# Two of the first four token tiles of x transposed by DMA instead of by TensorE

## The chip, the cores and the metric

The kernel runs on one core of a Trainium2 chip. The metric is the device time of one execution in microseconds (us); the time of the kernel before is the median of four runs, 180.27 us (180.03 to 180.73). A difference below about 0.3% (0.54 us) is not told from no change here.

## The reference

The inputs are in bf16: x with 2048 tokens of 512 features, wqkv (512 x 1536), wo (512 x 512), w1 and w3 (512 x 1376), w2 (1376 x 512) and gate_w (512). A linear-attention block and a gated feed-forward block work on the same x, and a gate per token mixes them:

```python
phi = lambda t: where(t > 0, t + 1, exp(t)) + 1e-6
q, k, v = heads(x @ wqkv)                       # 32 heads of 16
pq, pk = phi(q), phi(k)
kv = einsum("bhsd,bhse->bhde", pk, v)           # over all tokens
z = pk.sum(tokens)
a = (pq @ kv) / (pq . z + 1e-6) @ wo
b = (silu(x @ w1) * (x @ w3)) @ w2
g = sigmoid((x * gate_w).sum(-1))
out = g * a + (1 - g) * b
```

## The kernel before

The tokens are 16 tiles of 128 (t = 0 to 15), in four blocks of four tiles (`tb` = 0 to 3, `TB` = 512 tokens, `TPB` = 4). The 512 features are four chunks of 128 (`KC` = 4).

x is held twice in the on-chip memory. `x_sb` is token-major: a token's row lies in one partition. `xT` is feature-major: partition d of chunk kc holds feature kc*128+d of all tokens. A projection (k, q, the feed-forward) contracts over features and so reads `xT`. The product `XP` = x-transposed times phi(k), from which kv is made later, contracts over tokens and so reads `x_sb`.

All loads but one are issued by SP's queue, in the order of the program (L83 to L112). Before anything else come the token-major tiles 0-1 (L83), the second half of wk (L85; the first half goes by ACT's queue, L84) and the token-major tiles 2-3 (L86). Then, for each of the blocks 1 to 3, one DMA that reads 512 rows of x and writes them transposed into `xT` (L90), and one plain DMA that loads the same four tiles into `x_sb` (L94). After these come the weights wq, wr (the remainder of w1 and w3, and gate_w), wv, w1, w3, wo and w2 (L97 to L112). SP issues one after the other. Later SP issues small transposing DMAs between on-chip buffers (`hTr` L271: 128x128; `pqT` L295: 128x512, four of each per block), and the stores.

Block 0's `xT` isn't loaded. `emit_xT(t)` makes it for one tile: four 128x128 transposes on TensorE (PE, L174) into PSUM, then a copy of two chunks by VectorE (DVE, L179) and of two by ScalarE (ACT, L181).

Tiles 0-1, and tiles 2-3, are loaded in pairs: partition p of a pair holds the tokens 2p and 2p+1 of its 256 tokens, so that each partition's part is one run of 2 KB (`x_pairs`). The tokens of a pair of tiles therefore stand in another order in `x_sb`, `xT` and everything made from them, and the stores of tiles 0 to 3 put them back (`out_pairs`, L369).

TensorE's instructions are kept in the order of the program (L150). That order is: warm-up matmuls (L161); `emit_xT(0)` and `emit_xT(1)`; six matmuls of k for tiles 0 and 1 (L377); `emit_xT(2)` and `emit_xT(3)`; the ten matmuls left of k for tiles 1 to 3 (L382 to L385). Then, for t = 4 to 15 (L390 to L394), the four XP matmuls of tile t-4 alternate with the four k matmuls of tile t: XP(0), k(4), XP(1), k(5), XP(2), k(6) and so on. After k the q projections, the attention's small matrices, and the feed-forward blocks with the output matmuls follow to the end.

After each k tile comes `phi` (ACT L140, DVE L142 and L145) into `pk_sb`, and POOL adds the tile to a running sum (L192, L194). The four PSUM buffers of k ("mm") are taken again in turn, so k(4) needs what phi(k) of tile 0 leaves free.

Of the kernel before, what the change touches and what calls it, by code (L numbers as in the profile page):

```python
# [17 lines left out]
def kernel(  # L18
# [13 lines left out]
    P = nc.NUM_PARTITIONS  # L32
# [7 lines left out]
    TB = 512  # L40
    NTB = S // TB
    TPB = TB // P
# [6 lines left out]
    x2d = A_x.flatten_outer_dims()  # L49
    out2d = out.flatten_outer_dims()  # L50
# [13 lines left out]
    x_sb = consts.tile([P, NT, D], BF16, name="x_sb")  # L64
    xT = consts.tile([P, KC, S], BF16, name="xT")
# [12 lines left out]
    w3_r = B_w3.rearrange("(kc d) f -> d kc f", d=P)  # L78
    x_r = x2d.rearrange("(t p) d -> p t d", p=P)
    dq = nc.sync  # L80
    x_pairs = x2d[0:TB, :].rearrange("(g p j) d -> g p j d", p=P, j=2)
    out_pairs = out2d[0:TB, :].rearrange("(g p j) d -> g j p d", p=P, j=2)
    dq.dma_start(out=x_sb[:, 0:2, :], in_=x_pairs[0])  # L83
    nc.scalar.dma_start(out=wk_sb[:, 0:2, :], in_=wqkv_r[:, 0:2, D : 2 * D])  # L84
    dq.dma_start(out=wk_sb[:, 2:4, :], in_=wqkv_r[:, 2:4, D : 2 * D])  # L85
    dq.dma_start(out=x_sb[:, 2:TPB, :], in_=x_pairs[1])  # L86
    pre = consts.tile([1, 1], FP32, name="pre")
    nc.scalar.activation(out=pre[:], in_=nc.const_aps.tensor(0.0, [1, 1], FP32), func=ACT.Exp)
    for tb in range(1, NTB):
        dq.dma_start(  # L90
            out=xT[:, :, tb * TB : (tb + 1) * TB], in_=x2d[tb * TB : (tb + 1) * TB, :],
            transpose=True,
        )
        dq.dma_start(  # L94
            out=x_sb[:, tb * TPB : (tb + 1) * TPB, :], in_=x_r[:, tb * TPB : (tb + 1) * TPB, :]
        )
    dq.dma_start(out=wq_sb[:], in_=wqkv_r[:, :, 0:D])  # L97
    dq.dma_start(out=wr_sb[:, :, 0:FR], in_=w1_r[:, :, FM:F])
    dq.dma_start(out=wr_sb[:, :, FR : 2 * FR], in_=w3_r[:, :, FM:F])
    with nc.allow_non_contiguous_dma(reason="one gate weight per partition and chunk"):  # L100
        dq.dma_start(
            out=wr_sb[:, :, 2 * FR : NR], in_=gate_w.rearrange("(kc d o) -> d kc o", d=P, o=1)
# [7 lines left out]
    for fcs in (slice(0, FC // 2), slice(FC // 2, FC)):  # L110
# [9 lines left out]
        out=bm, in_=bm, pattern=[[-Dh, HPC], [0, Dh]], compare_op=ALU.is_ge, fill=0.0,  # L120
# [3 lines left out]
        out=bm, in_=bm, pattern=[[Dh, HPC], [0, Dh]], compare_op=ALU.is_ge, fill=0.0,  # L124
# [44 lines left out]
    def emit_xT(t):  # L169
        for h in range(2):  # L170
            xTp = psX.tile([P, 2, P], BF16, tag=f"XP{(2 * t + h) % 4}", name="xTp")
            for j in range(2):
                kc = 2 * h + j
                nc.tensor.transpose(  # L174
                    out=xTp[:, j, :], in_=x_sb[:, t, kc * P : (kc + 1) * P], identity=ident[:]
                )
            xT_t = xT[:, 2 * h : 2 * h + 2, t * P : (t + 1) * P]
            if h == 0:
                nc.vector.tensor_copy(out=xT_t, in_=xTp[:])  # L179
            else:  # L180
                nc.scalar.activation(out=xT_t, in_=xTp[:], func=ACT.Copy)  # L181
# [7 lines left out]
    def emit_k_phi(k_ps, t):  # L189
        e_ins = phi(pk_sb[:, t, :], k_ps[:])  # L190
        if t == 0:
            nc.gpsimd.tensor_copy(pks[:], pk_sb[:, t, :])  # L192
        else:
            nc.gpsimd.tensor_add(pks[:], pks[:], pk_sb[:, t, :])  # L194
# [137 lines left out]
    def emit_out(tb, tt):  # L332
        t = tb * TPB + tt
        tsl = slice(tt * P, (tt + 1) * P)

        if t < NT - 1:
            parts = [(0, D, True)]
        else:
            h, q3 = D // 2, 3 * D // 4
            parts = [(0, h, True), (h, q3, False), (q3, D, True)]  # L340
        o_out = work.tile([P, D], BF16, tag="o_out", name="o_out")
        lo = 0
        for i, (a, b, store) in enumerate(parts):
            o_ps = psX.tile([P, b - a], FP32, tag=f"XP{2 + (tt + i) % 2}", name="o_ps")
            for c in range(KC):
                nc.tensor.matmul(  # L346
                    o_ps[:], lhsT=st[tb, "pqT"][:, c, tsl], rhs=W_sb[:, c, a:b],
                    start=(c == 0), stop=False,
                )
            nc.tensor.matmul(  # L350
                o_ps[:], lhsT=st[tb, "hTr"][:FR, tsl], rhs=w2r_sb[:FR, a:b],
                start=False, stop=False,
            )
            for fc in range(FC):
                nc.tensor.matmul(  # L355
                    o_ps[:], lhsT=st[tb, "hT"][:, fc, tsl], rhs=w2_sb[:, fc, a:b],
                    start=False, stop=(fc == FC - 1),
                )
            if i < 2:
                nc.scalar.activation(  # L360
                    out=o_out[:, a:b], in_=o_ps[:], func=ACT.Copy, scale=omg[:, t : t + 1]
                )
            else:
                nc.vector.tensor_scalar(  # L364
                    out=o_out[:, a:b], in0=o_ps[:], scalar1=omg[:, t : t + 1], scalar2=None,
                    op0=ALU.mult,
                )
            if store:
                rows = out_pairs[t // 2, t % 2] if t < TPB else out2d[t * P : (t + 1) * P, :]  # L369
                nc.sync.dma_start(out=rows[:, lo:b], in_=o_out[:, lo:b])  # L370
                lo = b

# [4 lines left out]
    for kc, t in ((0, 0), (1, 0), (0, 1), (1, 1), (2, 0), (3, 0)):  # L377
        emit_k_mm(k0[t], t, kc)
    emit_k_phi(k0[0], 0)
    emit_xT(2)  # L380
    emit_xT(3)
    for t in range(1, TPB):  # L382
        for kc in range(2 if t == 1 else 0, KC):
            emit_k_mm(k0[t], t, kc)
# [30 lines left out]
    for c in range(KC):  # L415
# [7 lines left out]
        out=kvT_sb[:], in0=kvT_ps[:],  # L423
# [21 lines left out]
    for tb in range(NTB):  # L445
        for fc in range(FC if tb == 0 else 0, FC):
            emit_ffn(tb, fc)
        nx = tb + 1
        for tt in range(TPB):
            if nx < NTB:  # L450
                emit_q(nx, tt, psX, "XP0")
                if tt % 2 == 0:
                    emit_rem(nx, tt // 2, psX, "XP1")
            emit_out(tb, tt)
            if nx < NTB:
                emit_den(nx, tt)
        if nx < NTB:
            emit_norm(nx)
# [30 lines left out]
```

## Time and profile before

| | us |
|---|---|
| median of 4 runs | 180.27 (180.03 to 180.73) |
| the profiled execution, its own time | 180.06 |
| its span, first to last instruction | 178.3 |
| PE busy | 173.4 (97%), 876 matmuls |
| DVE busy | 119.2 (67%) |
| ACT busy | 66.4 (37%) |
| POOL busy | 63.2 (35%) |
| mean granted TensorE clock | 0.998 |

The span is what lies between the first and the last instruction; the profiled execution's time has another 1.76 us around it. PE's matmuls overlap: one of 512 columns is listed with 379 ns, but four of them end 0.86 us after the four before, so each takes 0.216 us of the stream. The profile's timeline gives the start of an instruction; the chain of work gives the stretch by which it moved the end, so the same matmul stands about 0.16 us later there. "PEld" are the loads of the stationary operand, which run ahead of the matmul. "SPq" lines are the issue of a DMA by SP's queue; how long the issue holds SP is their duration, and when the data has landed is given apart, counted from the start of the issue.

### The profile page before, as it was taken

The page shows a single profiled execution, that of the slowest core. Times are in us where ns is not written, and L with a number is a line of the kernel's source. Part 1 is how long each engine was busy: PE and PEld are TensorE (multiplying, and loading weights), DVE is VectorE, ACT ScalarE, POOL GpSimd, SP SyncE. Part 2 cuts the span into 40 slices and gives each one's busy share as a digit, 9 for nine tenths or more (in the row PEclk, how much of TensorE's full clock was granted, in tenths as well). Part 3 has the DMA queues.
Part 4 walks back from the last instruction along what each step waited for, and adds up shares of the span by engine and source line. Part 5 has one row for each costly group of instructions (what it writes and reads, how often), then busy time and mean ns, then how long its engine had stood idle before and what let it go on. Part 6 is the DMA issues. An engine that isn't in the chain of part 4 may idle for free.

```text
span 178.3 us, 2473 instructions
## 1 busy us (share of the span) xinstructions
PE 173.4 (97%) x876; PEld 83.9 (47%) x892; DVE 119.2 (67%) x205; ACT 66.4 (37%) x126; POOL 63.2 (35%) x71
## 2 busy tenths in 40 slices
PE   7999999999999999999999999999999999999993
PEld 3444444474444545444454544444545444444463
DVE  0678867998998737498786375978754669776000
ACT  3643324467532333343333333242433323341221
POOL 5196665767362323262003232620032328000000
PEclk9999999999999999999999999999999999999999
DMA  5999999931014010124000111240001022200011
GB/s 158 262 247 227 241 297 364 350 99 28 9 25 95 0 48 29 44 59 88 0 4 7 37 37 37 60 93 2 0 7 64 9 67 61 59 0 0 29 45 49
DMA packets 29085, 14.88 MB, mean 83 GB/s; under 512 B 19632, under 2 KB 28816, under 8 KB 29072
## 3 DMA queue, kind: packets, MB, share of 16 engines
q1 hardware_dynamic: 28800, 14.46, 30.3%
q10 hardware_dynamic: 272, 0.26, 0.5%
q8 instruction: 7, 0.11, 0.3%
q14 instruction: 6, 0.05, 0.1%
HBM read 8.42 MB, written 2.10 MB: 59 GB/s over the span
## 4 chain that ended last, share of the span: by engine, by line
PE 95%; DMA 2%; issue 1%; DVE 0%; DVEq 0%
PE gate_ps L310 19%; PE o_ps L355 19%; PE up_ps L318 19%; PE q_ps L217 8%; PE o_ps L346 8%; PE XP L204 8%; PE k_ps L184 6%; PE r_ps L241 3%; PE o_ps L350 2%; PE k L184 2%; DMA x_sb<-in_A_x_dram 2%; PE xTp L174 1%; PE kvT_ps L418 1%; PE W_ps L440 0%; DVE o_out L364 0%
## 5 line engine op out<-in xcount | busy, mean ns | idle before, releaser
L310 PE MATMUL gate_ps<-xT,w_sb 128*128 128x512 bf16 x157 | 40.9, 379 | 0.2
L318 PE MATMUL up_ps<-xT,w_sb 128*128 128x512 bf16 x156 | 40.7, 379 | 0.2
L225 POOL TENSOR_TENSOR qz<-pq,z_sb 128x512 f32<-128x512 bf16 x16 | 18.5, 1164 | 59.4 <-DVE pq L145 58.4
L323 ACT ACTIVATE th<-gate_ps 128x512 bf16<-128x512 f32 x40 | 23.9, 597 | 37.9 <-PE gate_ps L310 37.5
L355 PE MATMUL o_ps<-w_sb,hT 128*128 128x512 bf16 (+2 forms) x177 | 37.4, 354 | 0.2
L325 DVE SCALAR_TENSOR_TENSOR gs<-th,gate_ps 128x512 bf16<-128x512 bf16 x40 | 27.3, 682 | 5.6 <-ACT th L323 5.4
L328 DVE TENSOR_TENSOR hT<-up_ps,gs 128x512 bf16<-128x512 f32 x40 | 27.6, 691 | 3.7
L142 DVE TENSOR_SCALAR phi_m<-phi_e 128x512 bf16<-128x512 bf16 x32 | 15.0, 468 | 19.4 <-ACT phi_e L140 19.4
L355 PEld LDWEIGHTS <-hT 128*128 128x128 bf16 x180 | 16.8, 97 | 17.9
L318 PEld LDWEIGHTS <-w_sb 128*128 128x128 bf16 x160 | 15.7, 98 | 18.9
L310 PEld LDWEIGHTS <-w_sb 128*128 128x128 bf16 x160 | 15.6, 98 | 18.6
L360 ACT ACTIVATE o_out<-o_ps,omg 128x512 bf16<-128x512 f32 (+2 forms) x17 | 11.2, 656 | 30.4 <-PE o_ps L355 30.4
L290 POOL TENSOR_TENSOR pqn<-pq,rden 128x512 bf16<-128x512 bf16 x16 | 16.6, 1057 | 14.0 <-DVE rden L283 11.7
L194 POOL TENSOR_TENSOR pks<-pks,pk_sb 128x512 f32<-128x512 f32 x15 | 17.4, 1162 | 8.1 <-DVE pk_sb L145 7.6
L228 DVE TENSOR_REDUCE den<-qz 128x32 f32<-128x512 f32 x16 | 11.0, 684 | 8.4 <-POOL qz L225 8.3
L346 PE MATMUL o_ps<-W_sb,pqT 128*128 128x512 bf16 (+2 forms) x71 | 16.5, 355 | 0.0
L217 PE MATMUL q_ps<-wq_sb,xT 128*128 128x512 bf16 x61 | 16.3, 379 | 0.2
L204 PE MATMUL XP<-pk_sb,x_sb 128*128 128x512 bf16 x62 | 16.0, 379 | 0.1
L140 ACT ACTIVATE phi_e<-k_ps 128x512 bf16<-128x512 f32 x12 | 7.2, 597 | 14.4 <-PE k_ps L184 14.4
L140 ACT ACTIVATE phi_e<-q_ps 128x512 bf16<-128x512 f32 x16 | 9.6, 597 | 7.8 <-PE q_ps L217 7.8
L184 PE MATMUL k_ps<-wk_sb,xT 128*128 128x512 bf16 x48 | 12.3, 379 | 0.1
L145 DVE SCALAR_TENSOR_TENSOR pq<-q_ps,phi_m 128x512 bf16<-128x512 f32 x16 | 11.0, 690 | 0.5
(59 smaller groups left out, 119.0 us busy)
## 6 DMA issues: line engine op xcount, KB each, us to landing
w_sb<-in_B_w_dram SPq DMA_DIRECT2D x6, 640.0 KB, 9.1
out_dram<-o_out SPq DMA_DIRECT2D x15, 128.0 KB, 1.7
x_sb<-in_A_x_dram SPq DMA_DIRECT2D x3, 512.0 KB, 4.6
x_sb<-in_A_x_dram SPq DMA_DIRECT2D x2, 256.0 KB, 3.8
wq_sb<-in_A_wqkv_dram SPq DMA_DIRECT2D x1, 512.0 KB, 6.5
wv_sb<-in_A_wqkv_dram SPq DMA_DIRECT2D x1, 512.0 KB, 5.5
wo_sb<-in_A_wo_dram SPq DMA_DIRECT2D x1, 512.0 KB, 10.5
wk_sb<-in_A_wqkv_dram ACTq DMA_DIRECT2D x1, 256.0 KB, 3.9
```

Of the source, the lines that this page charges most:

```text
L184: nc.tensor.matmul(k_ps[:], lhsT=xT[:, kc, t * P : (t + 1) * P], rhs=wk_sb[:, kc, :], start=(kc == 0), stop=(kc == KC - 1),)
L194: nc.gpsimd.tensor_add(pks[:], pks[:], pk_sb[:, t, :])
L204: nc.tensor.matmul(XP_ps[dc][:], lhsT=x_sb[:, t, dc * P : (dc + 1) * P], rhs=pk_sb[:, t, :], start=(t == 0), stop=(t == NT - 1),)
L217: nc.tensor.matmul(q_ps[:], lhsT=xT[:, kc, ts_tok], rhs=wq_sb[:, kc, :], start=(kc == 0), stop=(kc == KC - 1),)
L225: nc.gpsimd.tensor_tensor(out=qz[:], in0=st[tb, "pq"][:, tt, :], in1=z_sb[:], op=ALU.mult)
L310: nc.tensor.matmul(gate_ps[:], lhsT=w1_sb[:, kc, fsl], rhs=xT[:, kc, tok_sl], start=(kc == 0), stop=(kc == KC - 1),)
L318: nc.tensor.matmul(up_ps[:], lhsT=w3_sb[:, kc, fsl], rhs=xT[:, kc, tok_sl], start=(kc == 0), stop=(kc == KC - 1),)
L323: nc.scalar.activation(out=th[:], in_=gate_ps[:], func=ACT.Tanh, scale=0.5)
L325: nc.vector.scalar_tensor_tensor(out=gs[:], in0=th[:], scalar=1.0, in1=gate_ps[:], op0=ALU.add, op1=ALU.mult)
L328: nc.vector.tensor_tensor(out=st[tb, "hT"][:, fc, :], in0=up_ps[:], in1=gs[:], op=ALU.mult)
L346: nc.tensor.matmul(o_ps[:], lhsT=st[tb, "pqT"][:, c, tsl], rhs=W_sb[:, c, a:b], start=(c == 0), stop=False,)
L355: nc.tensor.matmul(o_ps[:], lhsT=st[tb, "hT"][:, fc, tsl], rhs=w2_sb[:, fc, a:b], start=False, stop=(fc == FC - 1),)
```

## The change

The first pair of tiles keeps its load. Tiles 2-3 are no longer loaded token-major at the start: in that place SP issues a DMA that reads their 256 rows and writes them transposed into `xT`. Their token-major copy comes with block 1's, so that the first L94 load takes six tiles (2 to 7, 768 KB) instead of four. `emit_xT(2)` and `emit_xT(3)` go from PE's order, with their eight transposes, two DVE copies and two ACT copies. Tiles 2-3 now keep the tokens' own order, and so their stores are plain rows.

```diff
-    x_pairs = x2d[0:TB, :].rearrange("(g p j) d -> g p j d", p=P, j=2)
-    out_pairs = out2d[0:TB, :].rearrange("(g p j) d -> g j p d", p=P, j=2)
-    dq.dma_start(out=x_sb[:, 0:2, :], in_=x_pairs[0])
+    TF = 2
+    x_first = x2d[0 : TF * P, :].rearrange("(p j) d -> p j d", j=TF)
+    out_first = out2d[0 : TF * P, :].rearrange("(p j) d -> j p d", j=TF)
+    dq.dma_start(out=x_sb[:, 0:TF, :], in_=x_first)
     nc.scalar.dma_start(out=wk_sb[:, 0:2, :], in_=wqkv_r[:, 0:2, D : 2 * D])
     dq.dma_start(out=wk_sb[:, 2:4, :], in_=wqkv_r[:, 2:4, D : 2 * D])
-    dq.dma_start(out=x_sb[:, 2:TPB, :], in_=x_pairs[1])
     pre = consts.tile([1, 1], FP32, name="pre")
     nc.scalar.activation(out=pre[:], in_=nc.const_aps.tensor(0.0, [1, 1], FP32), func=ACT.Exp)
+    dq.dma_start(
+        out=xT[:, :, TF * P : TB], in_=x2d[TF * P : TB, :], transpose=True
+    )
     for tb in range(1, NTB):
         dq.dma_start(
             out=xT[:, :, tb * TB : (tb + 1) * TB], in_=x2d[tb * TB : (tb + 1) * TB, :],
             transpose=True,
         )
-        dq.dma_start(
-            out=x_sb[:, tb * TPB : (tb + 1) * TPB, :], in_=x_r[:, tb * TPB : (tb + 1) * TPB, :]
-        )
+        x_ts = slice(TF if tb == 1 else tb * TPB, (tb + 1) * TPB)
+        dq.dma_start(out=x_sb[:, x_ts, :], in_=x_r[:, x_ts, :])
...
-                rows = out_pairs[t // 2, t % 2] if t < TPB else out2d[t * P : (t + 1) * P, :]
+                rows = out_first[t] if t < TF else out2d[t * P : (t + 1) * P, :]
                 nc.sync.dma_start(out=rows[:, lo:b], in_=o_out[:, lo:b])
...
     emit_k_phi(k0[0], 0)
-    emit_xT(2)
-    emit_xT(3)
     for t in range(1, TPB):
```

## The prediction

> **What bounds the kernel now.** I read the page first, for which engine carries the span:
>
> ```profile
> span 178.3 us, 2473 instructions
> PE 173.4 (97%) x876; PEld 83.9 (47%) x892; DVE 119.2 (67%) x205; ACT 66.4 (37%) x126; POOL 63.2 (35%) x71
> PE 95%; DMA 2%; issue 1%; DVE 0%; DVEq 0%
> ```
>
> PE is busy from the first tile to the end and carries 95% of the chain. PE's order is fixed, so what shortens or stalls it early moves the end by the same time, unless a second wait swallows it. Next, the chain of work over the first 12 us:
>
> ```profile
> 0.81 3.24 DMA x_sb<-in_A_x_dram
> ...
> 4.77 1.47 PE k L184 x6
> 6.24 0.60 PE xTp L174 x8
> 6.83 2.16 PE k L184 x10
> 8.99 0.86 PE XP L204 x4
> 9.86 0.86 PE k_ps L184 x4
> ```
>
> The eight transposes that go are on the chain with 0.60 us. After them nothing stops PE: XP and k alternate, 0.86 us for each four matmuls. So I looked in the timeline at when the loads are issued (SP's lines) and when PE first needs them:
>
> ```profile
> 1.73 0.46 SPq L86 DMA_DIRECT2D x_sb<-in_A_x_dram  x1
> 2.23 3.69 SPq L90 DMA_TRANSPOSE xT<-in_A_x_dram  x1
> 5.96 0.58 SPq L94 DMA_DIRECT2D x_sb<-in_A_x_dram  x1
> 6.59 3.69 SPq L90 DMA_TRANSPOSE xT<-in_A_x_dram  x1
> ...
> 6.67 2.32 PE L184 MATMUL k<-wk_sb,xT 128*128 128x512 bf16 x10
> ...
> 9.69 1.03 PE L184 MATMUL k_ps<-wk_sb,xT 128*128 128x512 bf16 x4
> ...
> 12.28 1.03 PE L204 MATMUL XP<-pk_sb,x_sb 128*128 128x512 bf16 x4
> ```
>
> A transposing DMA of 512 rows holds SP for 3.69 us, six times the plain load of the same bytes (0.58), and what stands behind it on SP waits that long. The last line is XP(2), the first reader of tiles 2-3 in `x_sb` after the transposes. The landings, from the DMA issues (median, counted from the issue):
>
> ```profile
> x_sb<-in_A_x_dram SPq DMA_DIRECT2D x3, 512.0 KB, 4.6
> x_sb<-in_A_x_dram SPq DMA_DIRECT2D x2, 256.0 KB, 3.8
> pqT<-pqn SPq DMA_TRANSPOSE x16, 2.4
> xT<-in_A_x_dram SPq DMA_TRANSPOSE x3, 5.8
> ```
>
> Taken one by one, in narrow windows, the plain 512 KB loads land after 4.5, 4.6 and 5.7 us, the 256 KB ones after 3.2 and 4.4, and the three transposes after 5.7, 5.8 and 5.9.
>
> **The change part by part.** *PE transposes gone:* -0.60 us on the chain. The PE starts after them move up by as much: k(2)'s first matmul to 6.50 (6.67 - 0.60, and two matmuls of k(1) of 0.216 ahead of it), k(4) to 9.10, XP(2) to 11.68. With them go two DVE copies (292 ns each) and two ACT copies (381 ns each); they are worth nothing by themselves, since k(4) takes the PSUM buffer that phi of tile 0 gives up at 7.98 (DVE L145, 7.29 + 0.69), 1.1 us before 9.10. If phi came later than that they would count.
>
> A page of the Trainium skill speaks against the trade: "VectorE: DVE Perf Modes", the three transpose paths, gives a 128x128 transpose as 390 ns on TensorE and 1309 ns by DMA, and has TensorE as the choice where PSUM will do. By its 390 ns the part removed would be eight times that, 3.1 us; the trace has 0.60 for the eight, because they overlap, and the trace decides.
>
> *The transposing DMA of tiles 2-3, at 1.73 in place of the 0.46 us load:* the trace has no 256-row one. SP's hold is between the 1.22 us of a 128-row one (`pqT`) and the 3.69 of 512 rows. A line between the two gives 1.22 + 2.47/3 = 2.04, and I take that: same engine, same kind of block, twice one end and half the other. Its landing lies between 2.4 (`pqT`) and 5.8 us after issue, 4.1 to 7.5. It stands behind wk's second half, which lands at 5.47 (1.27 + 4.2), and 256 KB at the 290 GB/s that the windows show while a transpose alone runs are 0.9 us: 6.4, against k(2) at 6.50. Wait there: 0 to 1.0, taken 0.
>
> *Block 1's transpose* is then issued at 1.73 + 2.04 + 0.05 = 3.82 instead of 2.23, and at 5.8 lands at 9.6, against k(4) at 9.10: a wait of up to 0.5 us. In the trace it landed at 7.9 with k(4) at 9.69, so the 1.8 us of cover are spent, 0.6 on the earlier PE and 1.6 on SP. If the landing of 5.8 holds time queued behind the pair of tiles that is now gone, it is less: 0 to 0.5.
>
> *Block 1's token-major load* is issued at 3.82 + 3.69 + 0.04 = 7.55 instead of 5.96. It now holds six tiles, 768 KB, and XP(2) waits for all of it: the four early readers of tiles 2-3 are behind one DMA with tiles 4-7, whose own readers come two XP groups later. In the trace its landing (10.5) had XP(4) at 15.7 as first reader, 5 us of cover; tiles 2-3 had landed at 6.1. Its time to land: 4.5 us if the extra bytes cost nothing; plus 0.7 if they come at the best plain rate of the windows near it (some 350 GB/s), 5.2; plus 1.3 if they cost what 512 KB take above the lone first 256 KB (4.5 - 3.2), 5.8; 7.0 if it is as slow as the third one (5.7 + 1.3). I take 5.4, nearer to the two rates that fit the same load. Landing 7.55 + 5.4 = 12.95; PE starts 0.08 after a landing (L86 landed at 6.13, its transposes began at 6.21), so XP(2) is at 13.03 instead of 12.28: +0.75 us.
>
> The waits do not add. k(2), k(4) and XP(2) stand in one queue, and the last landing decides: a 0.5 us wait at k(4) moves XP(2)'s turn to 12.18, still before 13.03. Behind the waiting XP(2) stand all of PE's later work and so phi, the sums and all stores.
>
> Ends: fast, SP holds 1.22 and 4.5 to land, 1.73 + 1.22 + 0.05 + 3.69 + 0.04 + 4.5 = 11.23, before PE's turn: no wait, -0.60. Slow, 2.04 and 7.0: 14.55, +2.35; with 3.69 of hold another 1.65, +4.0, which would need 256 rows to cost as much as 512.
>
> "Advanced Engine Details and Errata", X-Bar Transpose (TRN2), says that transposing DMAs are as fast as regular ones. By that rule the new DMA would hold SP for the 0.46 us that it replaces, L94 would stay at 5.96, land at 11.4 by my 5.4, and the whole gain of 0.60 would stand; the row of 3.69 against 0.58 us says otherwise for the issue.
>
> *Later loads:* everything behind on SP is issued some 1.6 us later. Block 2's transpose: 6.59 + 1.7 + 5.8 = 14.1, and k(8) comes at 16.0 or later. wq lands at 22.1 and is first read at 30.4; gate_w and wv at 23.4 and 24.7, read at 36.5 and 37.8; the first halves of w1 and w3 at 27.3 and 29.1, read at 38.7 and 39.6; the last of w2 at 38.2, read at 59.6. The least cover is 8 us: nothing. If it were gone PE would wait there by the excess over 8. SP is done with loads at 31.8, and its next work is at 40.0, so `hTr` is not touched.
>
> *Stores of tiles 2-3:* as many, of the same size. Nothing; they start after 60 us, with SP mostly waiting.
>
> Sum: -0.60 + 1.35 wait = +0.75 on the profiled execution's 180.06 (its span of 178.3 and 1.76 around it), 180.81. It stands 0.21 below the median of 180.27, so the forecast is 181.0.
>
> **The rivals.**
> - *All hidden.* If SP's hold plus the time to land of the six tiles is at most 6.1 us (11.60 - 1.73 - 3.78), XP(2) does not wait. For it: 1.22 + 4.5 is 5.7, and the DMA engines have little behind them at 8 us. Against it: one row is a quarter of the source, the other has two thirds of the bytes. 180.27 - 0.60 = 179.7, on the other side.
> - *Only block 1's transpose is late.* `x_sb` lands in time, k(4) waits the 0.5 us: -0.1, 180.2. For it: 5.7 to 5.9 in three of three. Against it: `x_sb` comes after it on the same queue.
> - *The six tiles as slow as the third load.* 7.0 us to land, +1.8 to +2.35: 182.1 to 182.6. For it: one of three rows. Against it: that one ran beside the start of the weights.
>
> **How the numbers follow.** The late `x_sb`, 0.64: 180.4 to 181.7 around 181.0 (landing 5.2 to 5.8, hold 1.8 to 2.4 and a little either way); 0.12 of it is within 0.3% (0.54 us, about what a measurement of this kernel tells from no change). All hidden 0.12, of which 0.11 is faster by over 0.3%; only the transpose late 0.14, within; the slow load 0.10. Faster 0.11, same 0.27, slower 0.62. The range leaves a tenth on each side: from the whole gain, 179.7, to 182.2, in the slow load's case.
>
> **What the profile after would show.** Right: eight L174 matmuls instead of 16; the new transpose holding SP for about 2.0 us from 1.73; L94's first issue near 7.55; a PE wait for `x_sb` of about 1 us at XP(2), near 12 to 13; from there all PE starts 0.7 us late, to the end. Wrong: the hold is that of 128 rows or of 512; XP(2) starts without a wait; or PE waits for a weight near 38, where I count 8 us of cover.

## The result and the profile after

The changed kernel takes 179.80 us (median of 48, 179.15 to 180.45) against 180.21 beside it (73 runs): a ratio of 0.9970, interval 0.9962 to 0.9977, 0.4 us faster by the medians and 0.5 by the ratio. The forecast was 181.0 and slower. 179.80 lies inside the stated range, but on the side to which the prediction gave 0.11 for a clear gain and 0.27 for none. Single executions of either kernel differ by 1.3 us, mostly for a reason that the experiments found (PE's rate at the start, below), so a median of twelve is good to about 0.3 us. One execution of the changed kernel in a later batch took 478.19 us, with no other like it, and is left out of all figures.

The page of the changed kernel, the same two lines as before:

```profile
span 177.9 us, 2453 instructions
PE 172.9 (97%) x868; PEld 83.5 (47%) x884; DVE 118.6 (67%) x203; ACT 65.9 (37%) x124; POOL 63.2 (36%) x71
```

The span is 0.4 us shorter, PE is busy 0.5 less, and eight PE instructions are gone. The chain of work at the start (start, length, what):

```profile
1.73 4.96 DMA xT<-in_A_x_dram
6.69 0.05 issue
6.74 1.90 PE k L186 x8
8.63 0.86 PE XP L206 x4
9.50 0.86 PE k_ps L186 x4
```

The chain now goes through the new DMA: it lands at 6.69, and k(2) starts on it. After that nothing stops PE, as before. The timeline, SP's issues first and then PE's turns:

```profile
1.73 1.32 SPq L89 DMA_TRANSPOSE xT<-in_A_x_dram  x1
3.09 3.27 SPq L93 DMA_TRANSPOSE xT<-in_A_x_dram  x1
6.41 0.58 SPq L98 DMA_DIRECT2D x_sb<-in_A_x_dram  x1
7.04 4.12 SPq L93 DMA_TRANSPOSE xT<-in_A_x_dram  x1
...
3.79 0.62 PE L176 MATMUL xTp<-ident,x_sb 128*128 128x128 bf16 x8
4.46 1.90 PE L186 MATMUL k<-wk_sb,xT 128*128 128x512 bf16 x8
6.74 1.90 PE L186 MATMUL k<-wk_sb,xT 128*128 128x512 bf16 x8 [0.38 <-DMA xT<-in_A_x_dram]
8.47 1.03 PE L206 MATMUL XP<-pk_sb,x_sb 128*128 128x512 bf16 x4
...
11.93 1.03 PE L206 MATMUL XP<-pk_sb,x_sb 128*128 128x512 bf16 x3
```

and the landing of the six tiles, from the DMA issues:

```profile
x_sb<-in_A_x_dram SPq DMA_DIRECT2D x1, 768.0 KB, 5.0
```

The new DMA holds SP for 1.32 us, not 2.04. The one behind it holds SP for 3.27, less than the 3.69 of before. The six-tile load is issued at 6.41, only 0.45 later than the four-tile load of before, and lands at 11.4. XP(2) starts at 11.93 and waits for nothing. The wait that the profile does show is at k(2): PE was through with k(1) at 4.46 + 8 x 0.216 = 6.19 and stood for 0.55 us (the line has 0.38, counted from the listed end of the last matmul). XP(0) starts at 8.47 instead of 8.83, and that 0.36 us is the whole difference of the spans: from XP(0) to the end it is 169.4 us in this profile and 169.5 in that of before. The first transposes in the timeline of before:

```profile
4.10 0.62 PE L174 MATMUL xTp<-ident,x_sb 128*128 128x128 bf16 x8 [0.33 <-DMA x_sb<-in_A_x_dram]
```

They start 0.31 us later than in the profile after, where the first tiles landed 2.9 us after their issue instead of 3.2. So 0.31 of the 0.36 us is that landing, and only 0.05 is the 0.60 of the transposes less the 0.55 of the wait. This pair of profiles alone can't say what the change is worth.

So the predicted wait didn't come, and another one, costed at 0, did. The experiments ask what the transposes are worth, why SP was held so briefly, whether the predicted wait exists at all, and whether the wait at k(2) is a steady loss.

### The profile page after: what moved, and what is told of

It reads as the page before. It is cut to its first block, busy times and chain, and to the rows that moved or that the text cites. A ratio compares the mean times of both kernels' runs of the same rounds, so it can differ in the third digit from the quotient of the medians.

```text
span 177.9 us, 2453 instructions
## 1 busy us (share of the span) xinstructions
PE 172.9 (97%) x868; PEld 83.5 (47%) x884; DVE 118.6 (67%) x203; ACT 65.9 (37%) x124; POOL 63.2 (36%) x71
## 4 chain that ended last, share of the span: by engine, by line
PE 94%; DMA 3%; issue 1%; SPq 0%; DVE 0%; DVEq 0%
PE o_ps L357 19%; PE up_ps L320 19%; PE gate_ps L312 19%; PE o_ps L348 8%; PE XP L206 8%; PE q_ps L219 8%; PE k_ps L186 6%; PE r_ps L243 3%; DMA xT<-in_A_x_dram 3%; PE o_ps L352 2%; PE k L186 1%; PE kvT_ps L418 1%; PE W_ps L440 0%; SPq L86 0%; SPq L84 0%
```

## The experiments

**The transposes alone.** The kernel before, with `emit_xT(2)` and `emit_xT(3)` left out:

```diff
+    nc.gpsimd.memset(xT[:, :, 2 * P : TB], 0.01)
...
     emit_k_phi(k0[0], 0)
-    emit_xT(2)
-    emit_xT(3)
```

> The kernel before, with the PE transposes of tiles 2-3 and their copies left out and nothing else of the loads changed (xT of tiles 2-3 holds a constant, so k, q and the feed-forward of these tiles work on other numbers). Theory 1 (the gain is PE's own time for the eight transposes, 0.60 us on the chain): k(2) starts at 6.50 instead of 7.10, span 177.7, 0.6 us faster than before. Rival (the gain of the changed kernel comes from the loads, the first tiles landing at 3.7 instead of 4.05, and the transposes are worth little because PE then waits for something else near 6.2): k(2) stays near 7, 0 to 0.2 us faster.

Measured 179.48 us against 180.09, ratio 0.9972 (0.9957 to 0.9986): 0.5 us faster, with the loads untouched. The timeline of this kernel, PE:

```profile
3.68 1.06 PE L175 MATMUL xTp<-ident,x_sb 128*128 128x128 bf16 x8
4.53 3.98 PE L185 MATMUL k<-wk_sb,xT 128*128 128x512 bf16 x16
8.35 1.03 PE L205 MATMUL XP<-pk_sb,x_sb 128*128 128x512 bf16 x4
```

The transposes, with the copies that go with them, are the gain; the rival that gave it to the loads falls, since this kernel issues the loads of before. It is the median that carries this, not the profile, in which the first tiles happened to land early too (PE's first transposes at 3.68). XP(0) is at 8.35, though, not at the 8.23 that 8.83 - 0.60 gives, and here the eight transposes that are left take 1.06 us where the profile of before had 0.62. That needed an explanation, which comes below.

**Without the new DMA.** The changed kernel with a constant in its place:

```diff
-    dq.dma_start(
-        out=xT[:, :, TF * P : TB], in_=x2d[TF * P : TB, :], transpose=True
-    )
+    nc.gpsimd.memset(xT[:, :, TF * P : TB], 0.01)
```

> The changed kernel with the transposing DMA of tiles 2-3 left out (xT of these tiles holds a constant, so their k, q and feed-forward work on other numbers); SP's later loads start 1.4 us earlier. Theory 1 (the changed kernel loses about 0.5 us at k(2), waiting for that DMA, and nothing at XP(2)): k(2) starts at 6.2 instead of 6.74, no wait of PE for a DMA up to XP(2), 0.5 us faster than the changed kernel, 0.9 faster than before. Rival (the wait at k(2) is absorbed by a later one, at k(4) or XP(2)): as the changed kernel, within 0.2 us.

Measured 179.79, ratio 0.9981 (0.9964 to 0.9997). A miss: k(2) has nothing to wait for, and the time is the changed kernel's own; the fastest executions are alike too (179.21 here, 179.15 there). The wait of 0.55 us at k(2) is therefore no steady loss, as far as medians good to 0.3 us tell. The rival's reason for that, a later wait that takes it over, isn't there either: the profile shows no PE wait for a DMA, and XP(0) starts at 8.41.

**The same kernel again.** Each profile is one execution, so the changed kernel and the one before were run again, unchanged.

> The changed kernel once more, for another profile. Theory (PE's clock rises at a moment that the kernel doesn't set, and a wait at k(2) costs only where it rose early): if the first eight transposes take 0.62 us again, PE is at k(2) by 6.2 and waits for the new transposing DMA until it lands, 6.1 to 6.7; if they take about 1.03, PE gets to k(2) at 6.5 to 7 and waits little or nothing. XP(0) starts at 8.0 to 9.2, and the span is that plus 169.5 in either case. No wait at XP(2). Rival (the prediction's wait at XP(2) is there in some executions): a PE wait for x_sb near 12.

> The kernel before once more, for another profile: the first eight transposes at 0.62 or at about 1.03 us, as the clock has it; a 512-row transposing DMA holds SP between 3.2 and 4 us for the first, and differently from execution to execution for the later ones if the hold is a wait for room, the same within 0.1 if it is its own price.

> The changed kernel a third time, beside it: 179.6 to 180.0. SP is held 1.32 us by the 256-row DMA and 2.8 to 3.3 by the first of 512 rows; the load of tiles 2-7 is issued at 5.9 to 6.5 and lands after 5.0 to 5.2 us; the DMA of tiles 2-3 lands between 6.1 and 6.7; XP(0) starts at 8.0 to 9.0 and the span is that plus 169.5.

Medians of the changed kernel: 179.91 (eleven executions), ratio 0.9980 (0.9963 to 0.9997), and 179.47 (twelve; a little under what I expected), ratio 0.9961 (0.9944 to 0.9978). The timelines of PE at the start, second execution and third:

```profile
3.88 0.88 PE L176 MATMUL xTp<-ident,x_sb 128*128 128x128 bf16 x8
4.65 3.63 PE L186 MATMUL k<-wk_sb,xT 128*128 128x512 bf16 x16
8.12 1.03 PE L206 MATMUL XP<-pk_sb,x_sb 128*128 128x512 bf16 x4
```

```profile
3.81 1.03 PE L176 MATMUL xTp<-ident,x_sb 128*128 128x128 bf16 x8
4.63 4.52 PE L186 MATMUL k<-wk_sb,xT 128*128 128x512 bf16 x16
8.99 1.03 PE L206 MATMUL XP<-pk_sb,x_sb 128*128 128x512 bf16 x4
```

The same program starts XP(0) at 8.47, 8.12 or 8.99, and from there to the end it is 169.4 to 169.5 us in all three: what differs between these executions happens before. Two things move it. One is PE's rate. The line's own view, for the third execution, gives the range of single durations:

```profile
L176 PE MATMUL xTp<-ident,x_sb x8: 287/314/314, 3.8 to 4.5; 128*128 128x128 bf16 x8
L186 PE MATMUL k<-wk_sb,xT x16: 379/379/634, 4.6 to 8.8; 128*128 128x512 bf16 x16
```

A transpose takes 314 ns there and 219 in the profiles of before and after; a k matmul takes 634 ns at first and 379 later. Four slow ones make the third's k matmuls 4.52 - 3.63 = 0.89 us longer than the second's, so a slow one takes about 0.44 us of the stream, twice the 0.216. PE runs slower at the start and comes to its full rate at a moment that differs between executions: before the first transposes (profiles of before and after), during them (second execution), four matmuls into k (third, near 6.4 us). The profile's clock column says full speed for all these stretches and can't be used here; the durations can. The other thing is the landing of the new DMA: 6.69 in the first profile, 1.73 + 4.5 = 6.2 in both of these. PE got to k(2) at 6.39 and 7.26 (XP(0) minus eight matmuls of 0.216) and did not have to wait.

So PE waits at k(2) only where its rate rose early and the DMA landed late. In the first profile both were so; in the second and third there was no wait. That fits with the DMA's removal having gained nothing; how often the wait comes, three profiles can't say.

Block 1's 512-row transpose held SP for 3.27, 2.86 and 2.88 us in the three executions. In the kernel before run again, the three 512-row holds were 3.88, 3.50 and 3.54 us; in its first profile they were 3.69, 3.69 and 3.93. A price of the issue itself would repeat. What repeats in these profiles is where the holds end: shortly before the DMA queued directly ahead has landed. In the first profile of before they end at 5.92, 10.28 and 14.88 us, and the loads ahead land at 6.13, 10.46 and 14.92; in that of the changed kernel they end at 6.36, 11.16 and 15.25, against 6.69, 11.41 and 15.31. Block 1's hold began at 2.23 before and at 3.09 or 3.10 in the changed kernel's three profiles, and it ended at 5.92 and at 6.36, 5.96 and 5.97; without the new DMA, with 256 KB less ahead, it ended at 4.94. Whether SP waits for the landing itself or for room that it frees, no run separates.

**The hold, by itself.** Transposing DMAs into a scratch buffer were added to the changed kernel, of 512, 256, 128, 512, then 512, 512, 256 and 128 rows:

```diff
             emit_out(tb, tt)
+            for n in PROBES.get((tb, tt), ()):
+                nc.sync.dma_start(
+                    out=scr[:, st.setdefault("pi", 0) % 4, :, 0:n], in_=x2d[0:n, :], transpose=True
+                )
+                st["pi"] += 1
```

> The changed kernel with transposing DMAs of 512, 256 and 128 rows of x into a scratch buffer added behind the stores of the first blocks, microseconds apart, with nothing else queued, and once two of 512 rows back to back. Theory (how long a transposing DMA holds SP is its own issue time plus a wait for room behind what is already queued): alone, 512 rows hold SP for about 2.0 us, 256 for 1.3, 128 for 1.2; the second of the two back to back longer than the first. Rival (the prediction's: the hold is the issue's own price): 3.3 to 3.9 for 512 rows wherever it stands. The probes delay some stores; the time says nothing.

They did not come microseconds apart: SP's order put all eight together, from 31.55 on, behind the last weight loads. SP's issues:

```profile
31.55 5.65 SPq L461 DMA_TRANSPOSE scr<-in_A_x_dram  x1
37.24 1.30 SPq L461 DMA_TRANSPOSE scr<-in_A_x_dram  x1
38.59 1.27 SPq L461 DMA_TRANSPOSE scr<-in_A_x_dram  x1
39.90 2.10 SPq L461 DMA_TRANSPOSE scr<-in_A_x_dram  x1
42.12 2.95 SPq L461 DMA_TRANSPOSE scr<-in_A_x_dram  x1
45.16 2.73 SPq L461 DMA_TRANSPOSE scr<-in_A_x_dram  x1
47.98 1.26 SPq L461 DMA_TRANSPOSE scr<-in_A_x_dram  x1
49.34 1.22 SPq L461 DMA_TRANSPOSE scr<-in_A_x_dram  x1
```

The accident is useful. The same 512 rows hold SP for 5.65 us behind the weights, 2.10 behind two small ones, 2.95 and 2.73 behind another 512. The small ones cost 1.2 to 1.3 us in all four places. So the hold is no fixed price: it is at least the issue's own time, by these rows about 1.25 us up to 256 rows and about 2 for 512, and longer by a wait that depends on what is still queued. By that estimate the prediction's 3.69 was 2 of issue and 1.7 of waiting for DMAs that would have gone on anyway. How long the wait is behind a given queue is not settled: behind another 512 rows it is 0.7 to 0.9 us here and nothing in the next kernel.

**A later six-tile load.** The changed kernel with this load issued behind block 2's transpose:

```diff
     for tb in range(1, NTB):
         dq.dma_start(  # the block's rows, transposed
...
+        if tb == 1:
+            continue
+        if tb == 2:
+            dq.dma_start(out=x_sb[:, TF : 2 * TPB, :], in_=x_r[:, TF : 2 * TPB, :])
```

> The changed kernel with the token-major load of tiles 2-7 issued behind block 2's transposing DMA instead of ahead of it. Theory 1 (the load of the six tiles has 0.45 us to spare in the changed kernel, and once it is later PE waits for it at XP(2) one for one): the load is issued near 10.2 instead of 6.4, lands after 5.0 us at 15.2, XP(2) starts at 15.3 instead of 11.93: 3.4 us slower than the changed kernel, 3.0 slower than before. Rival (XP(2) does not decide, or the load lands faster when it is later): under 2 us slower.

Measured 182.15, ratio 1.0116 (1.0100 to 1.0131): 2.1 us slower than before. From its timeline, its waits and its DMA issues:

```profile
7.91 0.58 SPq L100 DMA_DIRECT2D x_sb<-in_A_x_dram  x1
...
14.22 1.04 PE L210 MATMUL XP<-pk_sb,x_sb 128*128 128x512 bf16 x3 [1.72 <-DVE pk_sb L151]
```

```profile
PEld L210 <- DMA x_sb<-in_A_x_dram: 2.2, 1, 2.2
```

```profile
x_sb<-in_A_x_dram SPq DMA_DIRECT2D x1, 768.0 KB, 6.3
```

The load is issued at 7.91, lands at 14.2, and XP(2) starts at 14.22 instead of 11.93. The timeline puts PE's wait down to a phi that ended at the same hundredth of a microsecond, but that phi is of tile 5, and XP(2) reads tile 2; the load of the stationary operand (PEld) names the DMA. So the wait that the prediction described exists, at its place. My expectation of 3.4 us on top of the changed kernel missed for the same cause as the prediction: I added a hold of 3.7 us for block 2's transpose, and both 512-row transposes together held SP for 4.76 (2.72, and 2.00 right behind it). Where the DMA decides, the executions agree: 181.98 to 182.20 over four, against spreads of 1.1 to 1.4 us elsewhere. That fits: a PE that waits later anyway loses nothing by a rate that rises late.

**Two DMAs of 128 rows.** The changed kernel with the 256 rows in two:

```diff
-    dq.dma_start(
-        out=xT[:, :, TF * P : TB], in_=x2d[TF * P : TB, :], transpose=True
-    )
+    for t in range(TF, TPB):
+        dq.dma_start(
+            out=xT[:, :, t * P : (t + 1) * P], in_=x2d[t * P : (t + 1) * P, :], transpose=True
+        )
```

> The changed kernel with the 256-row transposing DMA issued as two of 128 rows. Theory 1 (the hold on SP goes mostly by the number of DMAs, some 1.2 to 1.3 us each): SP is held about 2.5 us instead of 1.3, the load of x tiles 2-7 is issued at 7.6 instead of 6.4 and lands at 12.6, XP(2) starts at 12.7 instead of 11.93, 0.4 us slower than before: the wait of the prediction, with its hold; k(2) starts a little earlier, as it needs the first half alone, which changes nothing of the end. Rival (the hold goes by rows): 0.66 us each, the load of tiles 2-7 as in the changed kernel, k(2) earlier by 0.2 to 0.4 us and the end with it, 0.6 to 0.8 us faster than before.

> The two 128-row DMAs again. Open is why their median (180.12) lies 0.3 us above the changed kernel's although SP issued the load of tiles 2-7 no later (6.35) and PE waited for no DMA in the profile. Theory A (chance: the moment at which PE's clock rises fell late more often): the median comes out at 179.6 to 179.9, with the changed kernel run beside it. Theory B (the load of tiles 2-7 lands later, 5.8 us after its issue instead of 5.0, and stops XP(2) where the clock rose early): again 180.0 to 180.2, and if the profile has an early clock, a PE wait for x_sb of 0.3 to 0.7 us near 12.

Medians 180.12, ratio 0.9996 (0.9981 to 1.0012), and 180.20, ratio 0.9990 (0.9972 to 1.0008), the second beside the changed kernel's 179.47: no gain is seen any more. The second one's timeline and issues:

```profile
1.74 2.60 SPq L90 DMA_TRANSPOSE xT<-in_A_x_dram  x2
4.37 2.04 SPq L94 DMA_TRANSPOSE xT<-in_A_x_dram  x1
6.45 0.58 SPq L99 DMA_DIRECT2D x_sb<-in_A_x_dram  x1
...
12.09 1.04 PE L207 MATMUL XP<-pk_sb,x_sb 128*128 128x512 bf16 x4 [0.23 <-DMA x_sb<-in_A_x_dram]
```

```profile
x_sb<-in_A_x_dram SPq DMA_DIRECT2D x1, 768.0 KB, 5.6
```

As theory 1 had it, the hold goes by the number of DMAs: 2.60 for the two. But the next hold shrinks to 2.04, so the six-tile load is issued at 6.45, not 7.6; the issue was not where the time was lost. It lands after 5.6 us instead of 5.0 (5.8 in the first run), at 12.05, and here, where PE's rate rose early (XP(0) at 8.25), XP(2) stands for it: 12.09 instead of 8.25 + 3.46 = 11.71. In the first run the rate rose late, XP(2)'s turn was 12.66, and nothing waited. This is the predicted wait, 0.38 us of it instead of 1.35, and the changed kernel is 0.4 to 0.5 us away from it. Theory B holds as far as this goes: the wait is seen in one profile, and two batches of executions agree with it. Why the load takes 0.6 us longer to land, I can't say; block 1's transpose is issued 1.3 us later in this kernel and lands at 8.6 (4.37 + 4.2) against 8.0 (3.10 + 4.9) in the second execution of the changed one, so the queue ahead of the load is later by about as much.

**The six tiles in two loads.** In the same place, tiles 2-3 first:

```diff
+        if tb == 1:
+            dq.dma_start(out=x_sb[:, TF:TPB, :], in_=x_r[:, TF:TPB, :])
+            x_ts = slice(TPB, 2 * TPB)
         dq.dma_start(out=x_sb[:, x_ts, :], in_=x_r[:, x_ts, :])
```

> The changed kernel with the token-major load of tiles 2-7 issued as two DMAs in the same place, tiles 2-3 first and then 4-7. Theory (the six-tile load lands 0.4 to 0.5 us ahead of XP(2) and costs nothing): tiles 2-3 land 0.6 to 1 us earlier than the six did, at 10 to 10.5, PE takes no notice, the time is the changed kernel's within 0.2 us, 0.2 to 0.6 below before. Rival (the six tiles do stop PE in the executions whose clock rises early): 0.2 to 0.4 us faster than the changed kernel in the median, and its fastest execution below 179.0.

Measured 179.64, ratio 0.9976 (0.9961 to 0.9992). Tiles 2-3 landed at 6.03 + 3.1 = 9.1, two microseconds earlier, and PE took no notice: the six-tile load is not in the way. Up to 6 us this program is the changed kernel, so its profile also shows the new DMA once more: landed at 1.73 + 4.6 = 6.33, with PE's rate up early, a wait at k(2) of 0.16 us, XP(0) at 8.07. The DMA's own pace in that stretch, in windows of 0.5 us (start and end, length, granted clock, DMA share, GB/s), changed kernel and then this one:

```profile
5.50:6.00 0.50, 1.00 0.82 129
```

```profile
5.50:6.00 0.50, 1.00 1.43 276
```

In the first profile the transfers ran at half the pace there, which fits the landing at 6.69 instead of 6.2 to 6.3. What slowed them stays open.

**wk's second half by ACT's queue.**

```diff
-    dq.dma_start(out=wk_sb[:, 2:4, :], in_=wqkv_r[:, 2:4, D : 2 * D])
+    nc.scalar.dma_start(out=wk_sb[:, 2:4, :], in_=wqkv_r[:, 2:4, D : 2 * D])
```

> The changed kernel with the second half of wk issued by ACT's queue, behind the first half, so that SP's transposing DMA of tiles 2-3 is issued at 1.27 instead of 1.73 and is not behind wk. Theory (the wait at k(2) is the loss that is left): the DMA lands 0.3 to 0.6 us earlier, at 5.7 to 6.2, k(2) never waits, and the median falls by 0.1 to 0.2 us below the changed kernel, if wk's second half, needed at 5.3, doesn't come later. Rival (the two queues share the same DMA engines, so wk's half comes later by what the DMA gains): k(0) waits for wk instead, no gain or a loss of up to 0.5 us.

Measured 179.71, ratio 0.9976 (0.9959 to 0.9994); the changed kernel beside it 179.91 with an interval that overlaps it by far. The DMA was issued 0.47 us earlier and landed at 1.26 + 5.0 = 6.26, no earlier than the 6.2 to 6.3 of the others. The rival's price isn't there either: wk's second half landed at 1.30 + 4.0 = 5.30, where the changed kernel has 1.26 + 4.0 = 5.26. So an earlier place in the queue did not make the DMA land earlier, and what sets its landing stays open. On the time this run decides nothing.

**All of block 0 by DMA.** Tiles 0-1 transposed by SP's first DMA, wk by ACT's queue, no PE transposes:

```diff
-    dq.dma_start(out=x_sb[:, 0:TF, :], in_=x_first)
+    dq.dma_start(out=xT[:, :, 0 : TF * P], in_=x2d[0 : TF * P, :], transpose=True)
-    dq.dma_start(out=wk_sb[:, 2:4, :], in_=wqkv_r[:, 2:4, D : 2 * D])
+    nc.scalar.dma_start(out=wk_sb[:, 2:4, :], in_=wqkv_r[:, 2:4, D : 2 * D])
...
+    dq.dma_start(out=x_sb[:, 0:TPB, :], in_=x_r[:, 0:TPB, :])
...
-    emit_xT(0)
-    emit_xT(1)
```

> One step on: tiles 0-1 come transposed by DMA too, as SP's first DMA, both halves of wk go by ACT's queue, and tiles 0-3 come token-major in one load behind tiles 2-3's transposing DMA; PE makes no transposes. Theory (PE's transposes cost their time on PE, doubled while its clock is at half rate, and the loads cover what replaces them): tiles 0-1 land transposed at 4.0 to 4.3, k(0) starts at 4.3 to 4.6 instead of 4.5 to 4.7, tiles 2-3 land at 5.6 to 6.2, PE waits little, block 1's transpose (behind 1.5 MB) lands near 8.8 and may cost 0 to 0.4 at k(4): 0 to 0.4 us faster than the changed kernel. Rival (the first bytes are what everything waits for): tiles 0-1 land after 4.8, or k(4) waits over 0.5 us, and it is no faster than the changed kernel or slower.

Measured 183.13, ratio 1.0171 (1.0151 to 1.0191). The theory fell. The timeline of PE:

```profile
6.44 5.11 PE L187 MATMUL k<-wk_sb,xT 128*128 128x512 bf16 x16 [2.56 <-DMA xT<-in_A_x_dram]
11.38 1.03 PE L207 MATMUL XP<-pk_sb,x_sb 128*128 128x512 bf16 x4
```

Tiles 0-1 landed transposed at 6.4, 5.6 us after issue, where the plain load lands after 2.7 to 3.2. PE idled 2.56 us, and the sixteen k matmuls then took 5.11 us instead of 3.63, without another wait for a DMA: seven of them still ran at the slow rate, later than in any other kernel here. wk's second half, which the fifth k matmul reads, came later too, at 1.25 + 4.9 = 6.15 instead of 5.26; the wait that the profile shows is for the tiles. The same replacement that gains 0.4 us for tiles 2-3, which PE doesn't need before 6.2, loses 3.3 us against the changed kernel for the tiles that PE starts with.

## Why the prediction was wrong

- *"-0.60 us on the chain" for the eight transposes*: right. 0.5 us alone (0.9972, 0.9957 to 0.9986), with the loads of before.
- *SP's hold for 256 rows, "1.22 + 2.47/3 = 2.04"*: this step failed. It measured 1.31 to 1.32, in every profile of the changed kernel. I drew a line between 1.22 (128 rows) and 3.69 (512 rows) as if both were prices of the issue. By the estimate above the 3.69 held about 1.7 us of waiting behind other DMAs, and two other rows of the profile of before showed such waits, plain issues that take 0.5 us elsewhere:

```profile
16.65 1.91 SPq L99 DMA_DIRECT2D wr_sb<-in_B_w_dram  x1
23.75 2.21 SPq L108 DMA_DIRECT2D wo_sb<-in_A_wo_dram  x1
```

- *Block 1's transpose, 3.69 again*: the same step, a second time. It took 3.27, 2.86 and 2.88. A DMA put in front doesn't add its hold to a wait that counts from the queue's progress; it uses it up. That is why the six-tile load came at 6.0 to 6.4 instead of 7.55. The prediction had the number that was needed: it let the new DMA land at 6.4, and a hold that ends shortly before that landing gives just this.
- *Six tiles landing after 5.4 us*: 5.0 to 5.1. Nearly right, and a little under the lower of my two rates (5.2).
- *XP(2) at 13.03, +1.35 of wait*: it follows from the two holds. The load landed at 11.0 to 11.4 instead of 12.95, ahead of XP(2)'s turn, so the wait was 0. Both the place and the mechanism are real: put the load 1.5 us later and XP(2) waits until 14.22; cut the transposing DMA in two and XP(2) waits 0.4 us in an execution in which PE's rate rose early.
- *k(2), "0 to 1.0, taken 0"*: 0.55 in the first profile, 0 in the next two, and 0.16 in the kernel with the same start and two loads. The bounds held. The term could only be a distribution, since PE's arrival at k(2) is one.
- *"All hidden"* is the rival that came true, with its threshold: hold plus landing at most 6.1 us. It was 1.32 + 5.0 = 6.3 with a hold of 3.27 behind it instead of 3.69, so 5.9 by the threshold's own count. I gave it 0.12 because one of its two rows, `pqT`'s 1.22 us, seemed "a quarter of the source"; its 128 rows are half of the 256, and a quarter only of the 512. That row was nearly right. That 179.80 lies inside the stated range is no credit to the mechanism: the range's lower end, 179.7, was this rival's time.
- *"Only block 1's transpose is late"*: it was issued at 3.1 instead of 3.82 and landed after 4.9 to 5.4 us instead of 5.8, at 8.0 to 8.5 instead of 9.6, ahead of k(4) at 8.98 or later. The hold again, and a landing that counted time queued behind other DMAs.
- *Later loads, stores*: right. PE waits for no weight, and from XP(0) to the end nothing changed (169.4 us against 169.5).

On the pages cited. "VectorE: DVE Perf Modes" has TensorE ahead of the DMA for a transpose; measured here, the DMA wins where the data is needed late (0.4 us gained) and loses where it is needed first (3.3 us lost). "Advanced Engine Details and Errata", X-Bar Transpose (TRN2), has transposing DMAs as fast as regular ones; for the issue the runs have 1.32 against 0.46 us. What I drew from it, the six-tile load at 5.96 and the gain left standing, came closer than my 7.55 all the same (6.0 to 6.4). "TensorE: Matmul & The Clock Gate", Part 1, states that PE runs at half rate until a window of some 3.4 us was busy, that this window runs free of the kernel, and that the moment therefore varies. Rows of 634 and 379 ns, in changing numbers from one execution to the next, agree with a slow start that ends at a varying moment; no run here shows the window. The page's half a microsecond either way is less than the spread here, from before the first transposes at 3.8 us to the fourth k matmul near 6.4.

## What to carry to other kernels

How long a DMA's issue holds its queue is partly a wait for the DMAs ahead, so it must not be added up for a DMA that is inserted: take the shortest such row in an empty stretch as the price, and reckon landings from what is queued. The replacement by DMA paid here where the consumer came late; its margin is to be read at the first reader. Before a wait of half a microsecond near the start is costed from one profile, look at whether the first matmuls have the same duration in another one.

## What the runs showed that was not expected

PE's full rate starts at a moment that differs between executions of the same program, between 3.8 us (or earlier) and past 6 us. Between the second and third profiles of the changed kernel, neither of which waits for a DMA, XP(0) moves by 0.87 us, and the two executions differ by 0.86 (179.31 and 180.17); all its executions spread over 1.3. The program that waits for a DMA after that point varied by 0.2 over four. In the one kernel where PE idled for 2.56 us at the start, the rise came latest, past 9 us. And a transposing DMA of the same 512 rows held SP for anything between 1.95 us (behind the two of 128 rows) and 6.29 (behind the two token-major loads of the kernel with the later six-tile load).
